# Fewer word halves decoded in attention's tail, an earlier maximum and a separate strip buffer in a fused attention, expert and channel-mix kernel

## The chip, the cores and the metric

The kernel runs on one core of a Trainium2 chip. The time is the device time of one execution in microseconds (us). TensorE is PE, VectorE is DVE, ScalarE is ACT, GpSimd is POOL, SyncE is SP; a q behind a name (SPq, POOLq) is the engine as one that issues DMAs. A product is one PE instruction of a stationary 128 x 128 tile with up to 512 moving columns.

## What is computed

Three layers follow each other on 2 x 768 tokens of width 512. The attention is local (96 tokens back) with 8 global keys; the second layer sends each token to one of eight experts (a route by argmax, held over where a local gate is at least 0.5); the third is a channel mix. Cut from the reference:

```python
a = softmax(mask(scale * q @ k.T + bias))          # 2 x 8 heads x 768 x 64
x = (a @ v)                                        # 2 x 768 x 512
# experts: e chosen token by token
h = np.maximum(x[b, s] @ w1[e], 0.0)               # 512 x 1024
out[b, s] = p[e] * (h @ w2[e])                     # 1024 x 512
# channel mix
xk = mu_k * x + (1.0 - mu_k) * x_prev              # x_prev: token before
xr = mu_r * x + (1.0 - mu_r) * x_prev
k = np.maximum(xk @ w_k, 0.0)                      # 512 x 1024
v = k * k @ w_v                                    # 1024 x 512
r = 1.0 / (1.0 + np.exp(-(xr @ w_r)))              # 512 x 512
return r * v
```

The weights of the third layer, w_k, w_v and w_r, come as float64.

## The kernel before

**Products in three parts.** Every float32 operand of a product is split into a rounded part and a remainder (names that end in h or hi, and l or lo), and a product is made of three: hi x hi (L637), lo x hi (L638) and hi x lo (L639), by `mm3`. The rounded part is made by ACT, the remainder by DVE, which needs ACT's result. Weights: whi by ACT (L616), wlo by DVE (L622, L630). Activations that were turned on PE (L643): L645 on ACT and L646 on DVE. A wait of PE at L639 for a DVE split is thus a wait for the remainder.

**Words.** The float64 weights are read as pairs of 32-bit words. There are 20 pieces (`PIECES`), each half of one 128 x 1024 tile and 512 KB of words. `dec_load` (L741) asks POOL's DMA queue for a piece; `decode_fast` makes float32 of it in three DVE steps (L485, L487, L489). Pieces 0 and 1 are decoded early in attention. Pieces 2 to `TAILED` - 1 are decoded one step a call by `D_` while attention runs out, with three buffers in turn (dwa, qz, vp); when a piece is decoded, its buffer takes the next request. The other pieces are decoded by `B_` during the expert tiles, with two buffers of the tag dw (dwt in the rows). The results lie in z0, in the four slots of a large tile, zbig, and in four z tiles. The program's order on each engine is the order in which these calls are written; DVE and POOL take their instructions strictly in that order.

**Fill.** Attention's routing must be complete before any expert but those rows that are known already. So two tiles of the first expert are computed inside attention's tail by a generator `fl`, which `F_(m)` advances by m steps; `D_` calls stand between them. etb is the activation that turns up there between the expert's two products. At the end the third tile of the first expert is fetched as x0 by SP (L1221), turned and split into x0s.

**Expert tiles.** After attention come the first expert's third tile, experts 1 to 7 and, in the last of them, the preparation of block 0 of the channel mix. `W_` splits weights ahead, `B_` decodes words, and tables of numbers (`W0`, `B0`, `BL`, `WS`, `W7`) say how many steps stand behind each group of products.

**Channel mix.** `stage3` runs six blocks of 256 tokens. Per block: eight `k_step` (12 products of 256 columns into a bank S, squared by ACT and DVE: sq, kh, kl), two `r_unit` (products into PT, a sigmoid) and two `v_unit` (products into O, the output o). Before it, a block's gathered rows yg are scaled (L1332), turned by PE into a strip (one column of the token before, then 256 tokens) and mixed with the column before: `mix_a` on POOL, `mix_b` on DVE (L1366), then split into xrh and xrl, xkh and xkl (L1372 on ACT, L1376 on DVE). `early(u)` does this for block 0, at the steps u that `EARLY_AT` lists in the order scale, turn, scale, ra, rb, hi, lo, turn, ra, rb, hi, lo, ka, kb, khi, klo, khi, klo. The strips of even and odd blocks lie in slots 0 and 1 of zbig, where slot 0 also holds the word tile c = 0: its strip can be written only when that tile's remainder (wlo_0) has been taken.

**Check of the words.** In blocks 1 to 3 `find_small` reads all pieces once more and writes a minimum per piece into `n.low`. In block 4 at k_step 6 `small_w3` takes the maximum over the pieces on DVE (w3top, L495), turns it on PE (L497) and compares it (L499, L500) for the flag that chooses the general path.

Of the kernel before, what the change touches and what calls it, by code (L numbers as in the profile page):

```python
# [37 lines left out]
SHORT = (3, 5)  # L38
TAILED = 10
CAPS = [384, 256, 256 + LAST] + [256] * 5  # L40
# [9 lines left out]
WNEXT = (0, 0, 0, 1, 2, 1, 1, 2, 1, 1, 1, 1, 1, 0, 0, 0)  # L50
EARLY_AT = (7, 9, 11, 12, 12, 12, 14, 11, 13, 13, 13, 14, 13, 14, 16, 18, 16, 19)


class Net:
# [426 lines left out]
    def decode_fast(self, dst, src):  # L481
# [8 lines left out]
        yield  # L490

    def small_w3(self, pool):
        nc = self.nc
        top = pool.tile([P, 1], F32, name="w3top")
        nc.vector.tensor_reduce(top, self.low, axis=AX.X, op=ALU.max)  # L495
        tp = self.bank("R", 1)
        nc.tensor.transpose(tp[0:1, 0:P], top, self.ident)  # L497
        one = pool.tile([1, 1], F32, name="w3one")
        nc.vector.tensor_reduce(one, tp[0:1, 0:P], axis=AX.X, op=ALU.max)  # L499
        nc.vector.tensor_scalar(one, one, -F64_MIN ** 2, None, op0=ALU.is_gt)  # L500
        self.badi = pool.tile([1, 1], I32, name="badi")
        nc.vector.tensor_tensor(self.badi, self.bad, one, op=ALU.max)
# [63 lines left out]
def build(ctx, tc, ins, out):  # L566
# [163 lines left out]
    w3 = {nm: ins[nm].bitcast(U32) for nm in ("w_k", "w_v", "w_r")}  # L730
    ZS = KD * TB + 8
    zbig = zp0.tile([P, PAIRS, ZS], F32, name="zbig")
    strip = zbig[:, :, 0:S]
    WORD = (8, 9, 0, 1, 2, 3, 4, 5, 6, 7)
# [20 lines left out]
    ndw = [0]  # L755
    zs = [zbig[:, j, :] for j in range(4)]

    def zslot(k_, m):
        return zs[k_][:, 0:m]
# [222 lines left out]
    with tc.manual_schedule():  # L982
# [4 lines left out]
        n.setup()  # L987
        peb = [ap.tile([P, 2 * P], F32, name=f"peb{i}") if i % 2 else zbig[:, i // 2, S:S + 2 * P] for i in range(8)]
        qzz = ap.tile([P, 2 * PAIRS * P], F32, name="qz")
# [197 lines left out]
        n.route_ri(g[1], stat[g[1]][1])  # L1187
        F_(2)
        emit_pv(NI - 1, 0)
        emit_pv(NI - 1, 1)  # L1190
# [30 lines left out]
        nc.sync.dma_start(out=x0[0], in_=n.xs[bass.ds(row, P), :])  # L1221
        for _ in fl:
            D_(2)
        for _ in dgen:
# [8 lines left out]

    zs += [zp.tile([P, ZS], F32, name=f"z{j}") for j in range(4)]

# [95 lines left out]
    def scale(t):  # L1331
        nc.vector.tensor_scalar(yg[t], yg[t], n.PE[:, t:t + 1], 1.0, op0=ALU.mult, op1=ALU.mult)  # L1332

    def strip(b):
        if b not in strips:
            strips[b] = zslot(b % 2, KD * (TB + 1)).rearrange("p (a c) -> p a c", a=KD)
        return strips[b]
# [150 lines left out]
    def stage3():  # L1488
        small = small_words()
        for b in range(NB):  # L1490
            a, l = prep(b + 1) if b + 1 < NB else ([], [])
            if b == 0:
                gather(2)
                gather(3)
                for f in (KF + KF, KF + KF + 1):
                    early(f)
                for i in range(2):
                    r_unit(b, i)
                    early(KF + KF + 2 + i)
                    W_(4)  # L1500
            for f in range(KF):
# [7 lines left out]
                if b == 0:  # L1509
                    W_(2)  # L1510
                elif b < 4:
                    next(small, None)
                elif b == 4 and f == 6:
                    n.small_w3(rp)
# [15 lines left out]
    WS = (2, 1, 2, 1, 2, 1, 2, 1) + (2, 2, 2, 2, 1, 1, 1, 1)  # L1530
    BL = {1: ((0,) * 8, 9), 2: ((1, 1, 1, 0, 1, 1, 1, 0), 4), 6: ((1, 1, 1, 0, 1, 1, 1, 0), 2)}
    LATE = 4
    W0 = (0,) * 8 + (2, 2, 2, 2, 1, 1, 1, 1)
    B0 = (0, 0, 0, 0, 0, 0, 1, 0, 1, 0, 1, 1, 0, 1, 0, 1)
    W7 = ((1, 0, 0, 0, 2, 1, 2, 0, 1, 2, 2, 1, 1, 0, 0, 0), (0, 0, 0, 0, 0, 2, 2, 4, 0, 0, 0, 2, 2, 0, 2, 2))

# [337 lines left out]
```

## Time and profile before

| | |
|---|---|
| median of 3 runs | 521.3 us (520.7 to 522.87) |
| the profiled execution's own time | 519.15 us |
| its span | 517.2 us |
| PE busy | 487.6 us, 94% |
| weight loads of PE, beside it | 412.4 us, 80% |
| DVE busy | 347.1 us, 67% |
| ACT busy | 260.3 us, 50% |
| POOL busy | 130.6 us, 25% |
| read from and written to memory | 73.75 MB and 12.98 MB |

The profiled execution is one of its own, with a time of its own, some 2 us longer than the span of its instructions. The places of the kernel in that span: attention to about 140 us, its tail and the fill to 158, the expert tiles to about 326, then the channel mix. Times in the rows are from the start of the span. Matmuls overlap, so that busy times of neighbours run into each other; how close they follow is read from their starts.

### The profile page before, as it was taken

What the parts mean: (1) busy time and instruction counts of PE and PEld (TensorE: products, weight loads), DVE (VectorE), ACT (ScalarE), POOL (GpSimd) and SP (SyncE); (2) the same over time, 40 slices, a digit from 0 to 9 for tenths busy, and PEclk for the clock granted to TensorE, in tenths of its full rate; (3) what the DMA queues carried; (4) which work ended last, traced back from release to release, by engine and by line L of the source; (5) the groups of instructions that cost most, each with busy time, mean ns of one, the idle gap of its engine ahead of it and who ended that gap; (6) DMA issues with size and microseconds to landing.
All of it is one profiled execution on the core that took longest, in us unless ns stands there. A gap on an engine that the chain in (4) does not pass through costs nothing. (4 is left out here: it accounts for less than half of the span.)

```text
span 517.2 us, 9297 instructions
## 1 busy us (share of the span) xinstructions
PE 487.6 (94%) x3231; PEld 412.4 (80%) x3231; DVE 347.1 (67%) x885; ACT 260.3 (50%) x627; POOL 130.6 (25%) x225
## 2 busy tenths in 40 slices
PE   7999999989868999999999999789999999979995
PEld 4788888867647989867978988588989899878985
DVE  6768697977865775847887954887766768353301
ACT  4876867846314654647667655663433414133220
POOL 4101211561210000000000001724562918161220
PEclk8999999999989999999999999999999999989998
DMA  8987687666386966599689722101736441200101
GB/s 162 257 216 162 150 158 233 198 216 228 113 280 216 323 206 240 189 347 302 209 306 298 293 100 62 41 23 61 286 111 217 160 171 55 82 0 1 41 4 46
DMA packets 77128, 87.43 MB, mean 169 GB/s; under 512 B 50960, under 2 KB 51216, under 8 KB 77072
## 3 DMA queue, kind: packets, MB, share of 16 engines
q1 hardware_dynamic: 68304, 63.28, 40.0%
q0 software_dynamic: 4800, 16.78, 9.9%
q10 hardware_dynamic: 3968, 6.69, 3.5%
q8 instruction: 28, 0.46, 0.4%
q14 instruction: 28, 0.23, 0.1%
HBM read 73.75 MB, written 12.98 MB: 168 GB/s over the span
## 5 line engine op out<-in xcount | busy, mean ns | idle before, releaser
L616 ACT ACTIVATE whi<-wraw 128x512 fp32r<-128x512 f32 x124 | 70.1, 623 | 8.2 <-ACTq L699 2.6
L630 DVE TENSOR_TENSOR wlo<-wraw,whi 128x1024 fp32r<-128x1024 f32 x55 | 65.8, 1216 | 12.2 <-ACT whi L616 12.2
L1398 ACT ACTIVATE sq<-S 128x256 f32<-128x256 f32 x48 | 18.5, 385 | 83.8 <-PE S L639 81.3
L638 PE MATMUL S<-xkl,whi 128*128 128x256 f32 x192 | 54.7, 285 | 1.4 <-DVE xkl L1376 1.4
L637 PE MATMUL S<-xkh,whi 128*128 128x256 f32 x192 | 55.7, 290 | 0.0
L639 PE MATMUL S<-xkh,wlo 128*128 128x256 f32 x192 | 54.7, 285 | 0.0
L1408 POOL TENSOR_TENSOR kl<-sq,kh 128x256 fp32r<-128x256 f32 x40 | 34.9, 881 | 78.0 <-ACT kh L1407 78.0
L1438 DVE TENSOR_TENSOR o<-O,sig 128x512 f32<-128x512 f32 (+1 forms) x13 | 8.5, 650 | 55.7 <-PE O L639 34.1
L639 PE MATMUL O<-whi,kl 128*128 128x512 f32 (+1 forms) x104 | 39.4, 379 | 0.2 <-DVE kl L1408 0.2
L638 PE MATMUL O<-wlo,kh 128*128 128x512 f32 (+1 forms) x104 | 39.3, 377 | 0.0
L637 PE MATMUL O<-whi,kh 128*128 128x512 f32 (+1 forms) x104 | 39.2, 377 | 0.0
L638 PEld LDWEIGHTS S<-xkl,whi 128*128 128x128 f32 x192 | 36.8, 192 | 1.9 <-DVE xkl L1376 1.6
L637 PEld LDWEIGHTS S<-xkh,whi 128*128 128x128 f32 x192 | 36.7, 191 | 0.3
L639 PEld LDWEIGHTS S<-xkh,wlo 128*128 128x128 f32 x192 | 36.7, 191 | 0.0
L1399 DVE SCALAR_TENSOR_TENSOR sq<-S,sq 128x256 f32<-128x256 f32 x48 | 20.1, 421 | 18.7 <-ACT sq L1398 18.0
L741 POOL DMA_DIRECT2D dwt<-in_moe_w_v_dram x8 | 4.2, 530 | 92.0 <-DVE z L489 68.6
L883 ACT ACTIVATE pt<-PT 128x512 f32<-128x512 f32 (+1 forms) x24 | 13.4, 557 | 25.7 <-PE PT L876 23.6
L637 PE MATMUL O<-whi,hh 128*128 128x512 f32 x64 | 25.3, 396 | 0.0
L639 PE MATMUL O<-whi,hl 128*128 128x512 f32 x64 | 25.3, 395 | 0.0
L638 PE MATMUL O<-wlo,hh 128*128 128x512 f32 x64 | 25.2, 394 | 0.0
L1407 ACT ACTIVATE kh<-sq 128x256 fp32r<-128x256 f32 x48 | 19.7, 412 | 10.3 <-DVE sq L1399 10.3
L867 ACT ACTIVATE zbig<-zbig,nm 128x232 f32<-128x232 f32 (+1 forms) x48 | 22.4, 467 | 2.3 <-DVE nm L855 1.7
(435 smaller groups left out, 1453.4 us busy)
## 6 DMA issues: line engine op xcount, KB each, us to landing
wraw<-in_moe_w_dram SPq DMA_DIRECT2D x64, 512.0 KB, 6.0
dwt<-in_moe_w_v_dram POOLq DMA_DIRECT2D x8, 512.0 KB, 6.5
z<-in_moe_w_k_dram SPq DMA_DIRECT2D x8, 512.0 KB, 5.7
z<-in_moe_w_v_dram SPq DMA_DIRECT2D x8, 512.0 KB, 4.1
ys<-yo ACTq DMA_DIRECT2D x15, 256.0 KB, 5.1
xn<-xs SPq DMA_DIRECT2D x14, 256.0 KB, 4.2
vn<-in_v_dram SPq DMA_DIRECT2D x12, 256.0 KB, 5.7
kn<-in_k_dram SPq DMA_DIRECT2D x11, 256.0 KB, 5.3
```

Of the source, the lines that this page charges most:

```text
L616: nc.scalar.activation(out=whl[r, c][0][:, sl], in_=raws[r, c][:, sl], func=ACTF.Copy)
L630: nc.vector.tensor_tensor(lo, raws.pop((r, c)), hi.bitcast(F32), op=ALU.subtract)
L637: nc.tensor.matmul(out_, lhsT=ah, rhs=bh, start=first, stop=False)
L638: nc.tensor.matmul(out_, lhsT=ah, rhs=bl, start=False, stop=False)
L639: nc.tensor.matmul(out_, lhsT=al, rhs=bh, start=False, stop=last)
L867: nc.scalar.activation(out=pe, in_=pe, func=ACTF.Exp, scale=-1.0, bias=nm[:, h:h + 1], accum_out=sm[:, h:h + 1])
L883: nc.scalar.activation(out=d[:, 0:ps.shape[1]], in_=ps, func=ACTF.Copy)
L1398: nc.scalar.activation(out=sq_, in_=ps[:, 0:TB], func=ACTF.Relu)
L1399: nc.vector.scalar_tensor_tensor(sq_, ps[:, 0:TB], 0.0, sq_, op0=ALU.max, op1=ALU.mult)
L1407: nc.scalar.activation(out=hh, in_=sq_, func=ACTF.Copy)
L1408: (nc.gpsimd if b else nc.vector).tensor_tensor(hl, sq_, hh.bitcast(F32), op=ALU.subtract)
L1438: nc.vector.tensor_tensor(o[:, a:z], ps[:, 0:z - a], sig[b, i][:, a:z], op=ALU.mult)
```

## The change

Four things are changed together. `TAILED` goes from 10 to 7: pieces 7, 8 and 9 are no longer decoded in the tail, but by `B_` in the expert tiles, and the tables `B0`, `BL` and `W7` give those steps places; the calls of `D_` in the tail stand elsewhere (one `D_(2)` more near its start, then 0, 0, 1, 1 in turn at its end instead of 2 every time). The maximum of the word check becomes a function of its own, `small_top`, and is called in block 4 at k_step 1; the transposition stays at k_step 6. The strip of block 0 gets a buffer of the tag dw, strips of later blocks stay in zbig, which is now laid out with rows of 258 (257 columns are used), and `EARLY_AT` has new steps. In `stage3` two weight steps stand ahead of the r units of block 0, and five instead of four behind each.

```diff
-TAILED = 10
+TAILED = 7
-EARLY_AT = (7, 9, 11, 12, 12, 12, 14, 11, 13, 13, 13, 14, 13, 14, 16, 18, 16, 19)
+EARLY_AT = (7, 9, 8, 11, 12, 12, 12, 11, 12, 13, 13, 13, 13, 14, 16, 18, 16, 18)
...
+    def small_top(self, pool):
+        self.top = pool.tile([P, 1], F32, name="w3top")
+        self.nc.vector.tensor_reduce(self.top, self.low, axis=AX.X, op=ALU.max)
...
-        top = pool.tile([P, 1], F32, name="w3top")
-        nc.vector.tensor_reduce(top, self.low, axis=AX.X, op=ALU.max)
+        top = self.top
...
-    ZS = KD * TB + 8
-    zbig = zp0.tile([P, PAIRS, ZS], F32, name="zbig")
+    ZW = TB + 2
+    zbig = zp0.tile([P, PAIRS, KD, ZW], F32, name="zbig")
...
         F_(2)
+        D_(2)
         emit_pv(NI - 1, 0)
...
-        for _ in fl:
-            D_(2)
+        for j, _ in enumerate(fl):
+            D_((0, 0, 1, 1)[j % 4])
...
+    def strip_tile(b):
+        if b:
+            return zbig[:, b % 2, :, 0:TB + 1]
+        return mp.tile([P, KD, TB + 1], F32, tag="dw", bufs=2, name="strip0")
...
+                W_(2)
                 for i in range(2):
                     r_unit(b, i)
                     early(KF + KF + 2 + i)
-                    W_(4)
+                    W_(5)
...
+                elif b == 4 and f == 1:
+                    n.small_top(rp)
                 elif b == 4 and f == 6:
                     n.small_w3(rp)
...
-    BL = {1: ((0,) * 8, 9), 2: ((1, 1, 1, 0, 1, 1, 1, 0), 4), 6: ((1, 1, 1, 0, 1, 1, 1, 0), 2)}
+    BL = {1: ((0, 0, 0, 0, 1, 0, 1, 0), 4), 2: ((1, 1, 1, 0, 1, 1, 1, 0), 3), 6: ((1, 1, 1, 0, 1, 1, 1, 0), 2)}
...
-    B0 = (0, 0, 0, 0, 0, 0, 1, 0, 1, 0, 1, 1, 0, 1, 0, 1)
+    B0 = (0, 0, 0, 0, 0, 0, 0, 1, 1, 0, 0, 1, 1, 1, 1, 0)
```

**The end of the fill.** On DVE, before, from the remainder of the fill's last weight on (wlo_0; the zbig rows are word steps, and the word after the arrow is the buffer they read):

```order
L622 TENSOR_TENSOR wlo_0_2110<-wraw_0_1938,whi_0_2109 128x512
L485 TENSOR_SCALAR zbig<-vp 128x512
L487 SCALAR_TENSOR_TENSOR zbig<-vp,zbig 128x512
L489 SCALAR_TENSOR_TENSOR zbig<-vp,zbig 128x512
L485 TENSOR_SCALAR zbig<-dwa 128x512
L646 TENSOR_TENSOR etb_2104<-PT_2189,etb_2103 128x512
L487 SCALAR_TENSOR_TENSOR zbig<-dwa,zbig 128x512
L489 SCALAR_TENSOR_TENSOR zbig<-dwa,zbig 128x512
```

and further on, to the split of x0:

```order
L646 TENSOR_TENSOR etb_2104<-PT_2220,etb_2103 128x512
L485 TENSOR_SCALAR zbig<-dwa 128x512
L487 SCALAR_TENSOR_TENSOR zbig<-dwa,zbig 128x512
L489 SCALAR_TENSOR_TENSOR zbig<-dwa,zbig 128x512
L485 TENSOR_SCALAR zbig<-qz 128x512
L487 SCALAR_TENSOR_TENSOR zbig<-qz,zbig 128x512
L489 SCALAR_TENSOR_TENSOR zbig<-qz,zbig 128x512
L646 TENSOR_TENSOR x0s<-T_2246,x0s 128x512
```

After, on DVE, the same place in one piece:

```order
L625 TENSOR_TENSOR wlo_0_2113<-wraw_0_1938,whi_0_2112 128x512
L649 TENSOR_TENSOR etb_2107<-PT_2186,etb_2106 128x512
L489 SCALAR_TENSOR_TENSOR zbig<-vp,zbig 128x512
L485 TENSOR_SCALAR zbig<-dwa 128x512
L649 TENSOR_TENSOR etb_2107<-PT_2209,etb_2106 128x512
L487 SCALAR_TENSOR_TENSOR zbig<-dwa,zbig 128x512
L489 SCALAR_TENSOR_TENSOR zbig<-dwa,zbig 128x512
L649 TENSOR_TENSOR x0s<-T_2231,x0s 128x512
L485 TENSOR_SCALAR zbig<-qz 128x512
```

Both splits of etb now stand ahead of the steps that they followed, and the split of x0 ahead of the qz word instead of behind the words of vp, dwa and qz; line numbers are larger by three. On POOL, the requests for words (L741, then L745) among the scatters of rows (L277), before:

```order
L277 DMA xs<-X_1537,posi 12288x512
L277 DMA xs<-X_1710,posi 12288x512
L741 DMA vp<-in_moe_w_k_dram 128x1024
L277 DMA xs<-X_1852,posi 12288x512
L277 DMA xs<-X_2031,posi 12288x512
L741 DMA dwa<-in_moe_w_k_dram 128x1024
L741 DMA qz<-in_moe_w_k_dram 128x1024
L741 DMA vp<-in_moe_w_k_dram 128x1024
L741 DMA dwa<-in_moe_w_k_dram 128x1024
L741 DMA qz<-in_moe_w_k_dram 128x1024
```

and after:

```order
L277 DMA xs<-X_1537,posi 12288x512
L277 DMA xs<-X_1710,posi 12288x512
L745 DMA vp<-in_moe_w_k_dram 128x1024
L745 DMA dwa<-in_moe_w_k_dram 128x1024
L277 DMA xs<-X_1852,posi 12288x512
L277 DMA xs<-X_2034,posi 12288x512
L745 DMA qz<-in_moe_w_k_dram 128x1024
L745 DMA dwt_2266<-in_moe_w_k_dram 128x1024
```

The second request into dwa has moved ahead of the last two scatters; the last requests into vp, dwa and qz are gone, and requests into dwt follow instead.

**The start of block 0.** On DVE, before, from the last expert's weight w_9 on (xmr, xmk: mixing; xrl, xkl: remainders; wlo_0 to wlo_3: splits of word tiles; yg: scaling):

```order
L622 TENSOR_TENSOR wlo_9_4390<-w_9_1969,whi_9_4389 128x512 x2
L1332 TENSOR_SCALAR yg_4354<-yg_4354,PEX 128x512
L622 TENSOR_TENSOR wlo_0_4404<-zbig,whi_0_4403 128x512 x2
L646 TENSOR_TENSOR ehl_4360<-PT_4416,ehh_4359 128x512
L1332 TENSOR_SCALAR yg_4356<-yg_4356,PEX 128x512
L1366 SCALAR_TENSOR_TENSOR xmr_4450<-zbig,mur,xmr_4450 128x128 x4
L622 TENSOR_TENSOR wlo_1_4444<-zbig,whi_1_4443 128x512 x2
L1366 SCALAR_TENSOR_TENSOR xmr_4450<-zbig,mur,xmr_4450 128x128 x4
L1376 TENSOR_TENSOR xrl_4460<-xmr_4450,xrh_4459 128x4x128 x2
L1366 SCALAR_TENSOR_TENSOR xmk_4476<-zbig,muk,xmk_4476 128x256 x4
L622 TENSOR_TENSOR wlo_2_4491<-zbig,whi_2_4490 128x512 x2
L1376 TENSOR_TENSOR xkl_4507<-xmk_4476,xkh_4506 128x512
```

and after:

```order
L625 TENSOR_TENSOR wlo_9_4393<-w_9_1940,whi_9_4392 128x512 x2
L1337 TENSOR_SCALAR yg_4357<-yg_4357,PEX 128x512
L1337 TENSOR_SCALAR yg_4359<-yg_4359,PEX 128x512
L625 TENSOR_TENSOR wlo_0_4407<-zbig,whi_0_4406 128x512 x2
L649 TENSOR_TENSOR ehl_4363<-PT_4420,ehh_4362 128x512
L1376 SCALAR_TENSOR_TENSOR xmr_4445<-strip_4427,mur,xmr_4445 128x128 x4
L1386 TENSOR_TENSOR xrl_4464<-xmr_4445,xrh_4463 128x4x128
L1376 SCALAR_TENSOR_TENSOR xmr_4445<-strip_4427,mur,xmr_4445 128x128 x4
L1386 TENSOR_TENSOR xrl_4464<-xmr_4445,xrh_4463 128x4x128
L1376 SCALAR_TENSOR_TENSOR xmk_4480<-strip_4427,muk,xmk_4480 128x256 x4
L625 TENSOR_TENSOR wlo_1_4439<-zbig,whi_1_4438 128x512 x2
L1386 TENSOR_TENSOR xkl_4505<-xmk_4480,xkh_4504 128x512 x2
```

The split wlo_1 has moved from between the two groups of mixing for r to behind the mixing for k, each xrl follows its own mixing, and the second yg stands ahead of wlo_0.

**Block 4.** On DVE, before, from the sq of k_step 3 on:

```order
L1399 SCALAR_TENSOR_TENSOR sq_3_5774<-S_5761,sq_3_5774 128x256
L1399 SCALAR_TENSOR_TENSOR sq_4_5800<-S_5787,sq_4_5800 128x256
L1399 SCALAR_TENSOR_TENSOR sq_5_5822<-S_5809,sq_5_5822 128x256
L1366 SCALAR_TENSOR_TENSOR zbig<-zbig,muk 128x256 x4
L1399 SCALAR_TENSOR_TENSOR sq_6_5846<-S_5833,sq_6_5846 128x256
L495 TENSOR_REDUCE w3top<-w3low 128x1
```

and after, from the sq of k_step 0 on:

```order
L1409 SCALAR_TENSOR_TENSOR sq_0_5711<-S_5698,sq_0_5711 128x256
L1337 TENSOR_SCALAR yg_5714<-yg_5714,PEX 128x512
L1409 SCALAR_TENSOR_TENSOR sq_1_5733<-S_5720,sq_1_5733 128x256
L494 TENSOR_REDUCE w3top<-w3low 128x1
L1337 TENSOR_SCALAR yg_5716<-yg_5716,PEX 128x512
L1409 SCALAR_TENSOR_TENSOR sq_2_5756<-S_5743,sq_2_5756 128x256
```

The reduction to w3top stood behind the four mixing operations and the sq of k_step 6; now it stands behind the sq of k_step 1. The order of PE and of SP's requests is the same in both kernels.

## Rows read from the trace of the kernel before

**Rows 1.** Page, 40 slices of the span: clock and DVE in tenths, memory rate

```profile
PEclk8999999999989999999999999999999999989998
DVE  6768697977865775847887954887766768353301
GB/s 162 257 216 162 150 158 233 198 216 228 113 280 216 323 206 240 189 347 302 209 306 298 293 100 62 41 23 61 286 111 217 160 171 55 82 0 1 41 4 46
```

**Rows 2.** Waits of PE: total us, times, longest

```profile
PE O L639 <- DVE etb L646: 3.8, 2, 3.3
PE S L639 <- DVE x0s L646: 3.1, 1, 3.1
PE R L497 <- DVE w3top L495: 2.6, 1, 2.6
```

**Rows 3.** Timeline of PE, 138 to 158: start, us, instruction, [idle before]

```profile
141.36 0.39 PE L638 MATMUL O<-wlo,etb 128*128 128x512 f32 x1
145.09 0.50 PE L639 MATMUL O<-whi,etb 128*128 128x512 f32 x1 [3.33 <-DVE etb L646]
...
151.63 0.60 PE L643 MATMUL T<-ident,x 128*128 128x128 f32 x4
...
153.00 0.39 PE L638 MATMUL O<-wlo,etb 128*128 128x512 f32 x1
153.23 0.39 PE L639 MATMUL O<-whi,etb 128*128 128x512 f32 x1
...
157.22 0.50 PE L639 MATMUL S<-whi,x0s 128*128 128x512 f32 x1 [3.13 <-DVE x0s L646]
```

**Rows 4.** Timeline of DVE, 138 to 158

```profile
144.01 0.43 DVE L485 TENSOR_SCALAR zbig<-dwa 128x512 uint32<-128x512 uint32 x1 [2.40 <-DMA dwa<-in_moe_w_k_dram]
...
144.95 0.68 DVE L487 SCALAR_TENSOR_TENSOR zbig<-dwa,zbig 128x512 uint32<-128x512 uint32 x1
...
154.68 0.43 DVE L485 TENSOR_SCALAR zbig<-qz 128x512 uint32<-128x512 uint32 x1 [2.12 <-DMA qz<-in_moe_w_k_dram]
...
156.48 0.68 DVE L646 TENSOR_TENSOR x0s<-T,x0s 128x512 fp32r<-128x512 f32 x1
```

**Rows 5.** Timeline of ACT, POOL and SP's queue, 138 to 158

```profile
139.94 0.60 ACT L645 ACTIVATE etb<-PT 128x512 fp32r<-128x512 f32 x1 [1.22 <-PE PT L643]
138.62 0.58 POOL L741 DMA_DIRECT2D dwa<-in_moe_w_k_dram  x1
140.52 0.34 SPq L1221 DMA_DIRECT2D x<-xs  x1
```

**Rows 6.** DMA issues: count, KB each, median us to landing

```profile
wraw<-in_moe_w_dram SPq DMA_DIRECT2D x64, 512.0 KB, 6.0
dwt<-in_moe_w_v_dram POOLq DMA_DIRECT2D x8, 512.0 KB, 6.5
...
xn<-xs SPq DMA_DIRECT2D x14, 256.0 KB, 4.2
```

**Rows 7.** Timelines of PE, ACT and DVE at block 0

```profile
331.54 0.50 PE L639 MATMUL PT<-whi,xrl 128*128 128x512 f32 x1 [2.23 <-DVE xrl L1376]
339.17 0.38 PE L638 MATMUL S<-xkl,whi 128*128 128x256 f32 x1 [1.40 <-DVE xkl L1376]
334.77 1.28 ACT L1422 ACT_TABLE_LOAD   x1
340.57 0.42 DVE L1399 SCALAR_TENSOR_TENSOR sq<-S,sq 128x256 f32<-128x256 f32 x1
```

**Rows 8.** Timelines of DVE and PE at block 4

```profile
459.96 2.61 DVE L1366 SCALAR_TENSOR_TENSOR zbig<-zbig,muk 128x256 f32<-128x256 f32 x4
460.25 0.28 PE L639 MATMUL S<-xkh,wlo 128*128 128x256 f32 x1
...
466.76 0.39 PE L637 MATMUL PT<-whi,xrh 128*128 128x512 f32 x1
```

**Rows 9.** Waits of DVE in the expert tiles: total us, times, longest

```profile
DVE z L485 <- DMA dwt<-in_moe_w_v_dram: 1.8, 1, 1.8
```

More of the change, by code (lines that the diff above doesn't have):

```diff
@@ L730, in build @@
     w3 = {nm: ins[nm].bitcast(U32) for nm in ("w_k", "w_v", "w_r")}
-    ZS = KD * TB + 8
-    zbig = zp0.tile([P, PAIRS, ZS], F32, name="zbig")
-    strip = zbig[:, :, 0:S]
+    ZW = TB + 2
+    zbig = zp0.tile([P, PAIRS, KD, ZW], F32, name="zbig")
+    zflat = zbig.rearrange("p j a c -> p j (a c)")
+    strip = zflat[:, :, 0:S]
     WORD = (8, 9, 0, 1, 2, 3, 4, 5, 6, 7)
@@ L755, in build @@
     ndw = [0]
-    zs = [zbig[:, j, :] for j in range(4)]
+    zs = [zflat[:, j, :] for j in range(4)]
     def zslot(k_, m):
@@ L987, in build @@
         n.setup()
-        peb = [ap.tile([P, 2 * P], F32, name=f"peb{i}") if i % 2 else zbig[:, i // 2, S:S + 2 * P] for i in range(8)]
+        peb = [ap.tile([P, 2 * P], F32, name=f"peb{i}") if i % 2 else zflat[:, i // 2, S:S + 2 * P] for i in range(8)]
         qzz = ap.tile([P, 2 * PAIRS * P], F32, name="qz")
@@ L1232, in build @@
     TILES = [(2,), (0, 1), (0, 1, 2)] + [(0, 1)] * 5
-    zs += [zp.tile([P, ZS], F32, name=f"z{j}") for j in range(4)]
+    zs += [zp.tile([P, 1024], F32, name=f"z{j}") for j in range(4)]
     def xtile(shape, c, name):
@@ L1332, in scale @@
         nc.vector.tensor_scalar(yg[t], yg[t], n.PE[:, t:t + 1], 1.0, op0=ALU.mult, op1=ALU.mult)
+    def strip_tile(b):
+        if b:
+            return zbig[:, b % 2, :, 0:TB + 1]
+        return mp.tile([P, KD, TB + 1], F32, tag="dw", bufs=2, name="strip0")
     def strip(b):
         if b not in strips:
-            strips[b] = zslot(b % 2, KD * (TB + 1)).rearrange("p (a c) -> p a c", a=KD)
+            strips[b] = strip_tile(b)
         return strips[b]
@@ L1530, in build @@
     WS = (2, 1, 2, 1, 2, 1, 2, 1) + (2, 2, 2, 2, 1, 1, 1, 1)
-    BL = {1: ((0,) * 8, 9), 2: ((1, 1, 1, 0, 1, 1, 1, 0), 4), 6: ((1, 1, 1, 0, 1, 1, 1, 0), 2)}
+    BL = {1: ((0, 0, 0, 0, 1, 0, 1, 0), 4), 2: ((1, 1, 1, 0, 1, 1, 1, 0), 3), 6: ((1, 1, 1, 0, 1, 1, 1, 0), 2)}
     LATE = 4
     W0 = (0,) * 8 + (2, 2, 2, 2, 1, 1, 1, 1)
-    B0 = (0, 0, 0, 0, 0, 0, 1, 0, 1, 0, 1, 1, 0, 1, 0, 1)
-    W7 = ((1, 0, 0, 0, 2, 1, 2, 0, 1, 2, 2, 1, 1, 0, 0, 0), (0, 0, 0, 0, 0, 2, 2, 4, 0, 0, 0, 2, 2, 0, 2, 2))
+    B0 = (0, 0, 0, 0, 0, 0, 0, 1, 1, 0, 0, 1, 1, 1, 1, 0)
+    W7 = ((1, 0, 0, 0, 2, 1, 2, 0, 1, 2, 2, 1, 1, 0, 0, 0), (0, 0, 0, 0, 0, 2, 2, 2, 2, 0, 2, 0, 0, 0, 0, 2))
     with tc.manual_schedule():
```

## The prediction

> **What bounds the kernel now.** I read the page's slices first: TensorE (PE) is busy 94% of the span, so a microsecond is worth something only where PE waits. The clock row shows two levels, 9 (2.4 GHz) and 8 where a slice holds a stretch at the lower level (1.2 GHz); there are four: the first and the last of the span, the twelfth (142 to 155 us) and the thirty-sixth (453 to 465) [rows 1]. Next, the waits of PE, sorted by size: the three largest are a split of etb (3.8 us in two waits), a split of x0s (3.1) and w3top (2.6) [rows 2]. All three end on VectorE (DVE). Last, the timelines around these three places. They tell why DVE was late.
>
> In the tail of attention PE starts a product at 141.36 and the next at 145.09, and later stops again from 153.70 or so until 157.22 [rows 3]. DVE explains both stops. At 144.01 it starts the first step of a word half that it had waited 2.40 us for, and at 154.68 another that it had waited 2.12 us for; both waits end with a DMA [rows 4]. DVE works in order: behind the first stands the second half of the etb split, which takes its input from ScalarE (ACT), and ACT's half had started at 139.94 and takes 0.60 [rows 5], so it had been ready at 140.54, over 3 us before. The x0s split stands behind the second word at 156.48 [rows 4]. So PE waits for a transfer that it doesn't need for 100 us yet. The word for 144.01 was requested at 138.62 only [rows 5].
>
> In block 4 of the last stage PE starts a product at 460.25 and then the transposition of w3top, after 2.6 us of wait; the reduction that makes w3top stands on DVE behind four mixing operations that start at 459.96 and take 2.61 us together [rows 2, 8].
>
> **Part A, words moved out of the tail.** Removed from the tail: three of the eight word halves that are decoded there, that is nine DVE steps, each set 0.43 + 0.68 + 0.68 = 1.8 us (two fused steps, of which one stands here) [rows 4], 5.4 us in all, and three loads of 512 KB. More important is the order: etb's split now stands ahead of the word that DVE waited for, x0s' split ahead of the second such word, and the request for the first word stands two scatters earlier on the POOL queue.
>
> What PE needs there: from 141.36 to 157.22 it takes 15.86 us [rows 3]. In it are 25 products, the one at 141.36 counted and the one at 157.22 not, and two groups of four transpositions. At full clock products start 0.23 apart (153.00 and 153.23), and a group takes at most the 0.60 of its row [rows 3]. 25 x 0.23 + 2 x 0.60 = 6.95. So 15.86 - 6.95 = 8.9 us can go, and this holds the 3.3, 0.4 and 3.1 of waits and some 2 us that the products between 145.1 and 148.8 ran at the lower clock behind the first stop (the 8 in the twelfth slice).
>
> What is late next: x0 itself. Its load is issued at 140.52, in both orders at the same place [rows 5]. By the 4.2 us of loads of the same shape it lands at 144.7; by the 6.0 of the larger weights at 146.5 [rows 6]. PE transposes it in the group that now starts at 151.63 [rows 3]; between 141.36 and that group lie 17 products and the other group, without the stops 17 x 0.23 + 0.60 = 4.5 us, so PE is there at 145.9. x0 is in time by 1.2 or late by 0.6; I take it in time, since 4.2 is from the same shape and queue. Gain 8.9, between 7.5 (x0 late by 0.6 and as much again for a stretch at the lower clock behind that stop) and 9.4 (if a group takes 0.35).
>
> What the nine steps cost where they go: into the expert tiles, 155 to 297 us, where DVE's digits (slices 13 to 23) are 5 7 7 5 8 4 7 8 8 7 9, a mean of 0.68 [rows 1]. That leaves some 0.32 x 142 = 45 us of idle DVE for 5.4 us. I cost them at nothing. The cover is DVE's lead over PE: if a weight split is late by one step, PE stands 0.4 to 0.7 each time. Loads: 1.57 MB more in that stretch, at a mean 266 GB/s over these slices; single slices carry up to 347 [rows 1], so queues have room. Cost nothing, between 0 and the whole of it (rival 1).
>
> **Part B, the first strip in its own buffer.** Block 0 may be mixed before word tile c = 0 has been split, so the mixing of block 0 moves ahead of one split pair on DVE and of the second scaling. Two waits of PE are touched: xrl, 2.23 us at 331.54, and xkl, 1.40 us at 339.17 [rows 7]. The xrl split now comes directly behind its own mixing, so the first wait should shrink to nothing. But the gain is not kept: the third step of block 0 needs the bank that the first sq operation frees, at 340.57 [rows 7], and the work on DVE ahead of it is the same in kind and number in both orders (same splits, same mixing, same scalings, only permuted), with DVE at 8 tenths in slices 26 and 27, 323 to 349 us [rows 1]. PE arrives earlier and waits there. ACT adds the table load, 1.28 us at 334.77 [rows 7], which sits ahead of a sigmoid and two splits in both orders. I take 0.3 kept, between -1.0 (the load moves ahead of a split that PE waits for) and +2.2 (the whole xrl wait). Row stride 258 instead of 257 of the zbig tile changes no count: nothing.
>
> The table load is where the Trainium skill ("ScalarE: Activation LUTs", section "What ACT_TABLE_LOAD costs") says more than the row: 1.28 us of load plus 1.38 us of drain, 2.66 for a switch. The load's row agrees with the first figure; a drain has no row here. By the page's price the splits behind it would come 1.4 later and B would be about -0.2, an estimate that moves the sum by half a microsecond.
>
> **Part C, the maximum of the word check.** The reduction (0.16 us or so) goes from step 6 to step 1 of block 4, ahead of the second scaling; the transposition stays at step 6. Its input, the table of minima, is complete after block 3. From 460.25 to 466.76 PE takes 6.51 us [rows 8]. It holds 13 products of 256 columns, three of 512 and the transposition. At full clock: 13 x 0.12 + 3 x 0.23 + 0.2 = 2.45. Gain 4.06, of which 2.6 is the wait and the rest the products behind it at the lower clock. What is late next? The sq of step 6 stands behind the four mixing operations in both orders, but PE needs it only in the v units, with step 7 and the r units of the block before them. I take 4.1, between 3.5 and 4.2. Adding 0.16 us on DVE at step 1 costs nothing, since DVE idles between its operations there.
>
> **Sum.** -8.9 - 0.3 - 4.1 = -13.3 us on the profiled execution: 519.15 - 13.3 = 505.85. That execution lies 2.15 below the median of three (521.3); I keep the offset and predict 508.0.
>
> **The rivals.**
> 1. *The 1.57 MB in the expert tiles make weights late.* If queues there were already full, 1.57 MB at 266 GB/s adds 5.9 us where PE is bound: 508.0 + 5.9 = 513.9. For it: slices of 298 to 347 GB/s [rows 1], and weights of 512 KB that need 6.0 us to land [rows 6]. Against: the slices of 189 and 209 beside them. Chance 0.10.
> 2. *The strip's gain is kept.* B at 2.2 instead of 0.3: 506.1. For it: the wait of 2.23 is real. Against: DVE's full queue up to 340.57. Chance 0.08.
> 3. *C is not gained.* Another operation keeps PE at step 6, or the reduction at step 1 is itself late: 512.1. Chance 0.05.
> 4. *Slower: DVE stands at the words in the expert tiles as it stood in the tail.* By the tables the tiles of experts 0 to 2 now take 6 + 6 + 15 = 27 steps, nine words, where it was 6 + 2 + 12; each would wait like the two in the tail, 2.1 to 2.4 us [rows 4], in front of weight splits. 9 x 2.3 = 20.7 us: 508.0 + 20.7 = 528.7. With two buffers a word is requested when the one before the last is decoded, so it decides when a load takes longer than DVE needs for one word and the splits beside it, and by more than the split behind it is early. For it: loads of this kind need 6.5 us [rows 6], and one of the ten words of the expert tiles waited 1.8 us already [rows 9]. Against: only one did, and PE did not wait for it. Chance 0.05. The Trainium skill ("SBUF — State Buffer", section "Who interferes with whom") has a rule for it: DVE and POOL share a pair of ports as an exclusive lock, and transfers queued by POOL can be starved while DVE holds it. By that rule more DVE word steps beside POOL's word loads would lengthen the landing. The landing times of the rows, 6.5 us from POOL's queue and 6.0 from SP's for the same size [rows 6], show no such starvation, so the rule's case has no more than this chance.
> 5. *The gain of A comes back in the experts in another way*, so that the time stays within 0.5%: chance 0.02.
>
> **How the numbers follow.** Forecast 0.70. A from 7.5 to 9.4, B from -1.0 to 2.2, C from 3.5 to 4.2, and the median of three itself spreads 0.6 below and 1.6 above. All at their good ends at once is unlikely: 504.5 as the low end takes 3.5 from the forecast, rival 2 lies inside. The high end, 512.5, takes in rival 3 and B and A at their bad ends. Outside are rivals 1, 4, 5 and the tails of the forecast, together about 0.2. The bound of 0.5% (2.6 us) is about what a measurement of this kernel can tell from no change. Faster by over 0.5%: 0.93; within: 0.02; slower: 0.05.
>
> **What would show it.** In the trace after: (A) no wait of PE over 0.5 us at etb or x0s, the x0s products starting about 9 us earlier against 141.36's product, and a clock digit of 9 there; a wait of PE for the transposition of x by a DMA would show x0 late. (B) the wait for xrl gone, and in its place one for a bank freed by sq at an unchanged distance from the start of block 0; if the block's later products have also come nearer to its first one, rival 2. (C) no wait for w3top, and 13 small products 0.12 apart. Rival 1: PE waiting for wlo or whi in experts 1 to 4. Rival 4: DVE waits at L485 for words, several of 2 us. The forecast is wrong if the sum of PE's waits in the expert tiles grows by over 3 us.

## The result, and the profile after

| | before | after |
|---|---|---|
| median, this comparison | 521.69 us (520.7 to 522.87, 4 runs) | 501.62 us (499.54 to 504.26, 4 runs) |
| ratio, 95% interval | | 0.9617 [0.956, 0.9674] |
| profiled execution, its span | 519.15, 517.2 | 503.04, 501.0 |
| DVE busy | 347.1 (67%) | 345.6 (69%) |
| PE busy | 487.6 (94%) | 481.4 (96%) |

20.1 us were gained where 13.3 were forecast (508.0), and the median lies 2.9 below the low end of the range. Two later comparisons on other chips gave 0.9628 [0.9598, 0.9659] and 0.9638 [0.96, 0.9677]. So the direction was right and the size was not.

The three rows of the page that answer to [rows 1], from the profile of the changed kernel:

```profile
PEclk9999999999799999999999999989999999999999
DVE  6778788896766875967887964898675948364311
GB/s 159 273 199 189 126 185 175 258 225 132 228 188 227 346 218 319 190 334 315 212 339 308 284 148 45 61 22 63 222 157 154 246 87 166 64 21 1 42 3 47
```

The lower clock has moved: the digits below 9 stand now in the eleventh slice (125 to 138 us) and in the twenty-seventh (326 to 338); those at the etb split and at w3top are gone. The waits of PE from 310 us to 345 us are these (total, times, longest); none at etb, x0s or w3top is left in the whole list, and xrl has none:

```profile
PE S L640 <- ACT whi L619: 0.7, 1, 0.7
PE S L641 <- DVE xkl L1386: 0.7, 1, 0.7
PE O L642 <- DVE ehl L649: 0.3, 1, 0.3
PE S L642 <- DVE wlo L625: 0.2, 1, 0.2
```

**Tail of attention.** The timeline of PE, with the product that stood at 141.36 in [rows 3], the transposition of x, and the product that stood at 157.22:

```profile
143.45 0.39 PE L641 MATMUL O<-wlo,etb 128*128 128x512 f32 x1
...
147.81 0.60 PE L646 MATMUL T<-ident,x 128*128 128x128 f32 x4
...
150.11 0.40 PE L642 MATMUL S<-whi,x0s 128*128 128x512 f32 x1
```

The stretch of 15.86 us takes 6.66, no wait in it. DVE tells why (its timeline there):

```profile
142.66 0.69 DVE L649 TENSOR_TENSOR etb<-PT,etb 128x512 fp32r<-128x512 f32 x1 [0.94 <-ACT etb L648]
143.27 0.68 DVE L489 SCALAR_TENSOR_TENSOR zbig<-vp,zbig 128x512 uint32<-128x512 uint32 x1
143.87 0.42 DVE L485 TENSOR_SCALAR zbig<-dwa 128x512 uint32<-128x512 uint32 x1
145.87 0.69 DVE L649 TENSOR_TENSOR etb<-PT,etb 128x512 fp32r<-128x512 f32 x1 [1.58 <-ACT etb L648]
...
149.13 0.69 DVE L649 TENSOR_TENSOR x0s<-T,x0s 128x512 fp32r<-128x512 f32 x1 [1.25 <-ACT x0s L648]
149.74 0.42 DVE L485 TENSOR_SCALAR zbig<-qz 128x512 uint32<-128x512 uint32 x1
```

DVE now waits for ACT's half of each split instead of for words, the word out of dwa has landed by 143.87 without a wait, and x0s is split before the qz word.

**Block 4.** The last product ahead of the transposition of w3top (460.25 in [rows 8]), the transposition, and the product that stood at 466.76:

```profile
449.11 0.28 PE L642 MATMUL S<-xkh,wlo 128*128 128x256 f32 x1
449.22 0.27 PE L500 MATMUL R<-ident,w3top 128*1 128x128 f32 x1
...
451.45 0.40 PE L640 MATMUL PT<-whi,xrh 128*128 128x512 f32 x1
```

6.51 us have become 2.34.

**Where the rest is.** The order of PE is the same in both kernels, so the same products can be found in every trace, and the time between two of them be compared. The table gives six stretches: A is 141.36 to 157.22 in the trace of before, then to 328.57 (expert tiles), to 341.31 (start of block 0), to 460.25 (blocks 0 to 4), to 466.76 (C), to 508.95 (blocks 4 and 5). Kernels below the second line are the experiments.

| kernel | to 141.36 | A | experts | block 0 | blocks 0-4 | C | blocks 4-5 |
|---|---|---|---|---|---|---|---|
| before | 141.36 | 15.86 | 171.35 | 12.74 | 118.94 | 6.51 | 42.19 |
| after | 143.45 | 6.66 | 169.42 | 13.11 | 116.47 | 2.34 | 41.38 |
| top_only | 143.87 | 14.37 | 171.36 | 13.89 | 119.04 | 2.35 | 42.26 |
| tail_only | 143.34 | 7.29 | 170.89 | 12.71 | 119.08 | 6.60 | 42.18 |
| strip_only | 141.48 | 14.67 | 169.13 | 12.64 | 116.47 | 5.25 | 41.38 |
| pad64 | 144.74 | 15.51 | 169.35 | 12.72 | 116.78 | 6.67 | 41.78 |
| after_again | 144.82 | 6.66 | 168.83 | 12.63 | 116.41 | 2.34 | 41.38 |
| after_back | 141.12 | 6.66 | 170.68 | 12.60 | 119.04 | 2.35 | 42.25 |
| after_zbig | 141.02 | 7.36 | 169.10 | 12.07 | 116.45 | 2.34 | 41.39 |

Between before and after: A -9.2, C -4.2, block 0 +0.4, and three stretches in which the change was said to cost or gain nothing: experts -1.9, blocks 0 to 4 -2.5, blocks 4 and 5 -0.8, together -5.2 us. Ahead of all of it the after execution is 2.1 behind, by a stretch at the lower clock from 131 to 138 us (windows of PE in the trace of after: start and end, length, busy times, then the granted clock, DMA share and GB/s):

```profile
130.00:132.00 2.00, 1.84 (x12) 1.46 (x10) 1.44 (x4) 0.60 (x1) 0.00 (x0) 0.85 0.40 162
132.00:134.00 2.00, 2.00 (x11) 1.67 (x12) 1.70 (x10) 0.00 (x0) 0.47 (x1) 0.50 0.00 0
136.00:138.00 2.00, 2.00 (x7) 1.26 (x6) 1.20 (x5) 1.15 (x2) 1.46 (x2) 0.50 0.34 131
```

0.50 is the level of 1.2 GHz, 1.00 that of 2.4; ahead of it PE had waited 1.22 us for a step of the routing (er, at 129.30). The -5.2 come without any wait; they come a little at every product. A product's row names its moving operand first and its stationary one second: in the products of 256 columns the activations move and the weights stand, in those of 512 columns it is the other way round. In the two timelines below (before first, after second) stand the first of 48 products of 512 columns in block 3, the first of the 36 of 256 columns that follow them without a break, and the last of those:

```profile
438.30 0.39 PE L637 MATMUL O<-whi,kh 128*128 128x512 f32 x1
...
449.46 0.28 PE L637 MATMUL S<-xkh,whi 128*128 128x256 f32 x1
...
453.66 0.28 PE L639 MATMUL S<-xkh,wlo 128*128 128x256 f32 x1
```

```profile
427.77 0.39 PE L640 MATMUL O<-whi,kh 128*128 128x512 f32 x1
...
438.75 0.28 PE L640 MATMUL S<-xkh,whi 128*128 128x256 f32 x1
...
442.75 0.28 PE L642 MATMUL S<-xkh,wlo 128*128 128x256 f32 x1
```

Before: 11.16 us / 48 = 232.5 ns and 4.20 / 35 = 120 ns from start to start. After: 10.98 / 48 = 228.8 and 4.00 / 35 = 114. The clock is at its full level in both.

### The profile page after: what moved, and what is told of

Its sections match the earlier page's. It is cut to its first block, busy times and chain, and to the rows that moved or that the text cites. A ratio compares the mean times of both kernels' runs of the same rounds, so it can differ in the third digit from the quotient of the medians.

```text
span 501.0 us, 9283 instructions
## 1 busy us (share of the span) xinstructions
PE 481.4 (96%) x3231; PEld 408.6 (82%) x3231; DVE 345.6 (69%) x885; ACT 260.2 (52%) x627; POOL 131.2 (26%) x225
## 5 line engine op out<-in xcount | busy, mean ns | idle before, releaser
L1409 DVE SCALAR_TENSOR_TENSOR sq<-S,sq 128x256 f32<-128x256 f32 x48 | 20.1, 420 | 14.4 <-ACT sq L1408 14.1
L729 ACT ACTIVATE yo<-O 128x512 f32<-128x512 f32 (+1 forms) x16 | 9.5, 596 | 26.4 <-PE O L642 26.4
```

The lines of the kernel that those rows point to most:

```text
L1409: nc.vector.scalar_tensor_tensor(sq_, ps[:, 0:TB], 0.0, sq_, op0=ALU.max, op1=ALU.mult)
```

## The experiments

No kernel leaves out or changes any part of the computation. "Spacing" is the one of the two timelines above, in the same place of block 3 and 4.

### The parts alone, and the tiles moved

**top_only**: before, with part C.

```diff
+                elif b == 4 and f == 1:
+                    n.small_top(rp)
                 elif b == 4 and f == 6:
```

> The kernel before with part C alone (the maximum at k_step 1). Theory: the wait for w3top and the lower clock behind it go, 4.1 us less (ratio 0.990 to 0.994), and the pace of the products elsewhere stays that of before. Rival (PE is kept there by something else): 0 to 1.5 us less.

Measured: 516.65 us against 520.35, ratio 0.9936 [0.9906, 0.9966]. Stretch C 6.51 to 2.35, spacing 120 and 232 as before. The theory of part C holds: 3.7 us in the median, 4.2 in the stretch.

**tail_only**: before, with part A.

```diff
-TAILED = 10
+TAILED = 7
...
-        for _ in fl:
-            D_(2)
+        for j, _ in enumerate(fl):
+            D_((0, 0, 1, 1)[j % 4])
```

> The kernel before with part A alone (seven pieces in the tail, calls and tables as in the change), tiles in the places of before. Theory: 8.9 us less (7.5 to 9.4, ratio 0.982 to 0.986), all of it between 141 and 158 us, nothing given back in the expert tiles, pace of the products as before (119 ns for 256 columns). Rival (the products in the last stage are faster because words were moved): the changed pace, 113 to 114 ns, appears here, and the time falls by 13 to 14 us.

Measured: 512.06 against 520.35, 0.9836 [0.9791, 0.988], so -8.3. Stretch A 15.86 to 7.29; the expert tiles gave nothing back (171.35 to 170.89); spacing as before. The faster products are not an effect of the moved words.

**pad64**: before, with nothing but a wider slot for two buffers that the products never read.

```diff
-        return mp.tile([P, 1024], F32, tag="dw", bufs=2, name=f"dwt{ndw[0]}")
+        return mp.tile([P, 1028], F32, tag="dw", bufs=2, name=f"dwt{ndw[0]}")[:, 0:1024]
```

> The kernel before, and only the two dw buffers of the expert pool are declared 1028 instead of 1024 columns wide, of which 1024 are used: every tile that is placed behind them in that pool (xh, xl, hh, hl, xkh, xkl, xrh, xrl, kh, kl, the moving operands of the products) lies 64 bytes higher, as in the changed kernel. No instruction is moved. Theory (place of the tiles sets the pace of the products): products of 256 columns start 113 to 114 ns apart instead of 119, those of 512 columns 229 instead of 232, and the time falls by 4 to 6 us (ratio 0.988 to 0.992). Rival (the pace differs from run to run or chip to chip, or came with the strips or the words): spacing stays at 119, time within 1 us of before (ratio 0.998 to 1.002).

Measured: 514.63 against 520.35, 0.9903 [0.987, 0.9936], -5.7 us, with no instruction moved. Its timeline in the place shown above:

```profile
437.76 0.39 PE L637 MATMUL O<-whi,kh 128*128 128x512 f32 x1
...
448.74 0.28 PE L637 MATMUL S<-xkh,whi 128*128 128x256 f32 x1
...
452.74 0.28 PE L639 MATMUL S<-xkh,wlo 128*128 128x256 f32 x1
```

10.98 / 48 = 228.8 and 4.00 / 35 = 114 ns: the spacing of the changed kernel. Experts, blocks 0 to 4 and the end lose 2.0, 2.2 and 0.4 us. The buffer strip0 of 4112 bytes a row makes the two slots of the tag dw larger than the 4096 bytes of the words (the built program sets them 4128 apart), and all tiles placed behind them in the pool slide by 64 bytes; that is the missing term. The expectation calls xh to kl the moving operands; they are the activations of the products, moving with 256 columns and stationary with 512. Tiles that only other engines use slide with them (xn, yg and others), and no run separates whether the pace comes from PE's own reads or from what the other engines read and write beside them.

**strip_only**: before, with part B (buffer, rows of 258, early steps, weight steps).

```diff
+        return mp.tile([P, KD, TB + 1], F32, tag="dw", bufs=2, name="strip0")
```

> The kernel before with part B alone (own buffer for strip 0, rows of 258, early steps, weight steps of block 0 and the last expert as in the change). The buffer is 4112 bytes a row, so it moves the tiles by the same 64 bytes. Theory: it gains what the shift of the tiles gains, 4 to 6 us, and its own part is 0.3 us (-1 to 1): equal to the kernel with the shifted tiles alone. Rival (strip's gain kept): 2.2 us below the kernel with the shifted tiles alone. Rival (pace not by the place of tiles, but by the strip's rows of 258): gains 4 to 6 us where the shifted tiles alone gain nothing.

Measured: 511.62 against 520.35, 0.9864 [0.982, 0.9907]; 2.0 us below pad64 by the ratios (3.0 by the medians), but in the table the two differ by 0.1 in block 0. Most of what else they differ by lies ahead of A and in A and C, which neither touches, and where the executions differ in their stretches at the lower clock; strip_only has none behind its wait for w3top, pad64 has one. So the medians were no proof of a gain of the strip; this was tried again (after_zbig, zbig_mix).

### How the place of the tiles acts

Four kernels put a gap of so many bytes ahead of the expert pool of the kernel before, with one run each (the kernel before ran once beside them, at 519.67 us). With 128 bytes:

```diff
+    mp.tile([P, 32], F32, tag="gap", bufs=1, name="gap")
```

> The same with 32 bytes: operands at 32 modulo 64. If the place modulo 128 or 64 sets the pace: 119 ns or more, and the expert tiles' spacing for 512 columns at 232 or more.

> The kernel before with a gap of 128 bytes ahead of the expert pool, no instruction moved. Moving operands of the products then begin at 64 modulo 128, as in the kernel before (192 bytes past a multiple of 256 there, 64 past here). If the place modulo 128 sets the pace: 119 ns between products of 256 columns, as before. If any other place than that of before is fast: 113 to 114.

> The same with 192 bytes: operands at 0 modulo 128, but 128 modulo 256. If a multiple of 128 is enough: 113 to 114 ns. If a multiple of 256 or more is wanted: 119.

> The same with 320 bytes: operands at 0 modulo 256, but 256 modulo 1024. If a multiple of 128 or 256 is enough: 113 to 114 ns. If only 1024 (the bytes that one product of 256 columns reads in a partition) will do: 119.

Then, in the changed kernel, a gap of 192 bytes that takes the activations back to the residue of before, that is to the same place modulo 256 (**after_back**), and a gap ahead of the weights that moves these by 192 bytes, with one of 64 that brings the activations back to a multiple of 256 (**after_wgap**):

```diff
+    wp.tile([P, 48], F32, tag="gapw", bufs=1, name="gapw")
...
+    mp.tile([P, 16], F32, tag="gap", bufs=1, name="gap")
```

> The changed kernel with a gap of 192 bytes ahead of the expert pool, so that the operands of the products begin again 192 bytes past a multiple of 256, as in the kernel before; no instruction is moved. Theory (their place sets the pace): 119 and 232 ns again, and 4 to 6 us longer than the changed kernel. Rival (the pace came with the changed order): 113 to 114 ns, same time within 1.5 us.

> The changed kernel with the weight tiles (whi, wlo, wraw) moved up by 192 bytes, from 64 past a multiple of 256 to a multiple of 256, the moving operands staying at multiples of 256. If only the place of the moving operands counts: 113 to 114 and 229 ns, same time within 1.5 us. If the distance between weights and moving operands counts (then equal, as with the gap of 128): 120 ns for 256 columns and 227 for 512, some 2 us longer. If weights at a multiple of 256 are better by themselves: below 113 or 227 ns, 2 to 4 us shorter.

What these texts call moving operands are the activations, in either role. In the table the distance is where activations begin, less where weights begin, modulo 256, as the built programs place them (weights begin 64 past a multiple of 256, in after_wgap at one). Counted as the moving operand's place less the stationary one's, it is this distance with 256 columns and minus this distance with 512.

| kernel | distance | 512 columns, ns | 256 columns, ns | time |
|---|---|---|---|---|
| before, after_back | 128 | 232.5 | 120 | after_back 505.06 us, 0.9721 [0.9675, 0.9767] |
| shift32 | 160 | 233.3 | 117 | 522.25 us, one run |
| after, pad64, shift320 | 192 | 228.8 | 114 | shift320 516.10 us, one run |
| shift128, after_wgap | 0 | 226.7 | 120 | shift128 516.74 us, one run; after_wgap 503.15 us, 0.9675 [0.9635, 0.9716] |
| shift192 | 64 | 233.3 | 118 | 521.71 us, one run |

after_back's timeline, in the same place, shows the spacing of before in the changed order:

```profile
428.15 0.39 PE L640 MATMUL O<-whi,kh 128*128 128x512 f32 x1
...
439.31 0.28 PE L640 MATMUL S<-xkh,whi 128*128 128x256 f32 x1
...
443.51 0.28 PE L642 MATMUL S<-xkh,wlo 128*128 128x256 f32 x1
```

and after_wgap's that the weights' place counts too:

```profile
426.87 0.39 PE L641 MATMUL O<-whi,kh 128*128 128x512 f32 x1
...
437.75 0.28 PE L641 MATMUL S<-xkh,whi 128*128 128x256 f32 x1
...
441.94 0.28 PE L643 MATMUL S<-xkh,wlo 128*128 128x256 f32 x1
```

The simple expectation of shift192 (a multiple of 128 will do) falls, and so does the one that only the activations' own residue counts: the activations of after and after_wgap both begin at multiples of 256, and 256 columns take 114 in one and 120 in the other. In this place kernels with the same distance agree in both columns; as a rule that rests on one pair, shift128 and after_wgap, since in the other rows of several kernels activations and weights each lie at the same places modulo 256. after_back stands 0.0093 of the kernel before above the changed kernel's 0.9628 on the same chip, 4.8 us (3.2 between the medians of six runs each); its stretches in the table say 5.4 (1.9 + 2.6 + 0.9).

**after_mix**: the changed kernel with kh, kl, hh, hl (512 columns) at distance 0 and the other operands at 192, to have the better of both rows.

```diff
+        mp.tile([P, 16], F32, tag="gapa", bufs=1, name="gapa")
         hn = [mp.tile([P, D], F32, tag="h" + c, bufs=5, name=f"hn0{c}") for c in "hl"]
+        mp.tile([P, 48], F32, tag="gapb", bufs=1, name="gapb")
```

> The changed kernel with two gaps in the expert pool: hh, hl, kh, kl (operands of 512 columns of the second products) lie 64 bytes past a multiple of 256, as the weights do, and xh, xl, xkh, xkl, xrh, xrl stay at multiples of 256. Theory (distance from the weights modulo 256: 192 is best for 256 columns, 0 for 512): 113 to 114 ns for 256 columns as in the changed kernel, 227 instead of 227 to 232 for O products by hh, hl, kh, kl; some 454 products by 2.5 ns, 1.1 us shorter. Rival (one pool's place governs all): 120 ns for 256 columns, 2 us longer.

> The changed kernel unaltered, beside the two above on their chip: 0.960 to 0.966 of the kernel before.

Measured: 502.22 us, 0.9654 [0.9627, 0.9682], beside 501.15, 0.9638 [0.96, 0.9677] for the changed kernel (after_third). The products by kh and kl took 227 ns as expected, but those of 256 columns 118 in the place of the timelines (means of 115 to 118 from block to block), with their distance modulo 256 unchanged. No gain.

So the distance is not the whole of it, and two other kernels of this record show more. In pad64 and after_zbig (described below) every operand of every product of the channel mix lies at the same address. In the place of the timelines their spacing is the same, 228.8 and 114 ns. Further on, in blocks 4 and 5, it is not: here are the first of 48 products of 512 columns, and the first and the last of 96 of 256 columns that follow them without a break, pad64 first and after_zbig second.

```profile
470.72 0.39 PE L637 MATMUL O<-whi,kh 128*128 128x512 f32 x1
...
481.70 0.28 PE L637 MATMUL S<-xkh,whi 128*128 128x256 f32 x1
...
492.89 0.28 PE L639 MATMUL S<-xkh,wlo 128*128 128x256 f32 x1
```

```profile
453.24 0.40 PE L640 MATMUL O<-whi,kh 128*128 128x512 f32 x1
...
464.44 0.28 PE L640 MATMUL S<-xkh,whi 128*128 128x256 f32 x1
...
475.23 0.28 PE L642 MATMUL S<-xkh,wlo 128*128 128x256 f32 x1
```

pad64: 10.98 / 48 = 228.8 and 11.19 / 95 = 117.8 ns. after_zbig: 11.20 / 48 = 233.3 and 10.79 / 95 = 113.6. The granted clock is 1.00 in both. Among the kernels with all activations at distance 192, those with a stretch at the lower clock shortly before, in block 4 (in pad64 the granted clock is 0.89 from 455 to 470 us, in after_zbig 1.00 from 440 to 455), take 229 and 118 ns here (pad64, shift320), and those without take 233 and 114 (strip_only, after, after_zbig): what PE did before seems to count, which is read from these traces and not tried. So the place of the tiles sets the pace only in part, for both sizes; what else counts stays open.

### Whether the strip's buffer gains

**after_again** is the changed kernel unaltered, for comparison; **after_zbig** is the changed kernel with strip 0 in zbig again, early and weight steps as before, and the slots of dw kept wide, so that the tiles stay where they are; **zbig_mix** is that with the gaps of after_mix.

```diff
     def strip_tile(b):
-        if b:
-            return zbig[:, b % 2, :, 0:TB + 1]
-        return mp.tile([P, KD, TB + 1], F32, tag="dw", bufs=2, name="strip0")
+        return zbig[:, b % 2, :, 0:TB + 1]
```

> The changed kernel unaltered, on the chip and beside the kernels it is compared with here. Expected: 0.960 to 0.967 of the kernel before; the sum of the parts measured alone (words -8.3, maximum -3.7, strip with its shift of the tiles -8.7 us) is -20.7, so 499.5 to 503. If the parts overlapped, less: 503 to 507.

> The changed kernel without part B alone: strip 0 in zbig again, early steps and weight steps of block 0 and of the last expert as before; the tiles stay where the changed kernel has them. If the strip's own part is worth what was predicted (0.3 us, -1 to 1): within 1.3 us of the changed kernel. If its gain is kept (xrl wait of 2.2 us, and the stretch at the lower clock behind it of 1.7 us in some executions): 2 to 4 us longer.

> The same gaps in the changed kernel without part B (strip 0 in zbig). Theory: 1 to 2 us shorter than the changed kernel, for the places 1.1 and for the strip left out 0 to 1. Rival (strip's own part gains): longer than the kernel with the gaps and the strip by 1 to 3 us.

Measured: after_again 501.91, 0.9628 [0.9598, 0.9659], as the parts add up (0.0164 + 0.0064 + 0.0136 less than 1 is 0.9636). after_zbig 500.63, 0.9611 [0.9574, 0.9647]; zbig_mix 499.62, 0.9629 [0.959, 0.9669], against after_mix 0.9654. Both times the kernel without part B is 0.2% lower, inside the intervals; in the table its block 0 takes 12.07 against 12.63 us. The strip's buffer has no gain of its own. The two kernels without it are as fast as the changed one; none is shown to beat it.

## Why the prediction was right or wrong

**Part A, right.** Forecast 8.9, measured 9.2 in the stretch, inside 7.5 to 9.4, and 8.3 alone. x0 came in time: no wait ahead of the transposition at 147.81. The nine steps cost nothing in the expert tiles: PE waits there for no split. One word wait is longer than in [rows 9] (waits of DVE, 150 to 316 us, after):

```profile
DVE z L485 <- DMA dwt<-in_moe_w_v_dram: 4.6, 1, 4.6
```

so rival 4 has its mechanism, once, at a place where DVE had the time. The rule of the Trainium skill ("SBUF — State Buffer", section "Who interferes with whom"), by which transfers that POOL queues can be starved, does not show here: words from POOL's queue landed in 5.4 us (w_v) and 6.9 (w_k), weights from SP's in 5.8.

**Part B, right in kind, and in size by luck.** Forecast -0.3; measured +0.4 in the first profile, which has a stretch at the lower clock there (0.67 from 328 to 332 us), and -0.1 in after_again, which has none. The wait for xrl is gone and the one that was named, for the bank that the first sq frees, stands in its place, beside the halved one for xkl (1.40 in [rows 7]) and one for whi that was not named, in the waits of PE of after_again from 310 to 345 us:

```profile
PE S L640 <- ACT whi L619: 0.7, 1, 0.7
PE S L641 <- DVE xkl L1386: 0.7, 1, 0.7
PE S L640 <- DVE sq L1409: 0.7, 1, 0.7
```

That sq starts 12.2 us after the product that begins the stretch, where it was 12.0 before (340.57 in [rows 7], less 328.57). But after_zbig, without part B, has the wait for xrl, and yet takes 12.07 us instead of 12.63:

```profile
PE PT L642 <- DVE xrl L1384: 1.8, 1, 1.8
```

There that sq starts after 11.4 us. So the strip's buffer with its order cost 0.6, and something else, which the prediction put at nothing, gave about as much (below); the -0.1 is what was left of the two.

As for the drain that the Trainium skill ("ScalarE: Activation LUTs", section "What ACT_TABLE_LOAD costs") adds to the table load: after loads from 326.51 to 327.79, and the sigmoid starts at 327.80. The load's 1.28 us agree, no drain shows in the timeline of ACT here:

```profile
326.51 1.28 ACT L1432 ACT_TABLE_LOAD   x1
327.80 0.60 ACT L1432 ACTIVATE sig<-PT 128x512 f32<-128x512 f32 x1
```

**The step that failed: part B was priced by the order of its instructions alone.** The new buffer got no price for its size, and the layout of zbig got "Row stride 258 instead of 257 of the zbig tile changes no count: nothing." I looked at the instructions that a buffer's size changes and not at what is placed behind it. The new 4112-byte strip in a slot of 4096 moves the activations of nearly all products of the expert tiles and the channel mix by 64 bytes, while the weights stay where they were, worth 5.2 us in the trace and 5.7 alone. (zbig itself kept its size, 4 x 258 = 4 x 256 + 8, and moved nothing.) No term of the sum and no bound held it; a price for "all tiles behind it move" would have had to be there, as an unknown of either sign (shift32 and shift192, at 522.25 and 521.71 beside 519.67, were not faster than before, by one run each).

The other half of that step is smaller: with zbig declared in four dimensions, POOL's mixing of the first half of block 0 no longer stops behind its first operation for the second transposed half, which it doesn't read. tail_only's POOL first (flat rows), after_zbig's second (rows of 258):

```profile
317.59 0.38 POOL L1362 TENSOR_SCALAR xmr<-zbig,mur 128x128 f32<-128x128 f32 x1 [0.73 <-ACT zbig L1347]
319.18 3.53 POOL L1362 TENSOR_SCALAR xmr<-zbig,mur 128x128 f32<-128x128 f32 x7 [1.21 <-ACT zbig L1347]
```

```profile
313.97 4.13 POOL L1369 TENSOR_SCALAR xmr<-zbig,mur 128x128 f32<-128x128 f32 x8 [0.63 <-ACT zbig L1354]
```

From the start of the stretch, POOL is done with these eight operations after 1.2 us in tail_only and after 0.6 in after_zbig, about what block 0 gained. That the 12.07 us of after_zbig come from it is argued from these rows, and from pad64 and tail_only, whose block 0 gains nothing (12.72 and 12.71); it was not tried alone.

**Part C, right.** Forecast 4.1, measured 4.2 in the stretch, 3.7 alone.

**The offset, mis-sized.** I kept the 2.15 us between the profiled execution and the median. The one of after lies 1.4 above its median, that of before 2.5 below the later median of 521.69: 4.0 us between them. Stretches at the lower clock can account for that: they come behind a stop of PE, and not in every execution behind the same (in the table, top_only has one in block 0 and takes 13.89 us there, tail_only has none and takes 12.71). In the comparison with after_again the mean granted clock was 0.9805 over 11 runs of before and 0.9947 over 6 of the changed kernel, (0.0195 x 519) - (0.0053 x 501) = 7.5 us of clock loss less, if PE had work all that time; the sum held two stretches of it, some 3.4. That the stops which were removed had triggered more of it, on average, than the one profile of before showed, is argued: beside 0.9835 for the kernel before, the mean is 0.9888 with part A alone and 0.9856 with part C alone.

Together: 13.3 + 5.2 (tiles) + 4.0 (offset) - 2.1 (lower clock ahead of A in the profile of after) - 0.7 (block 0) + 0.4 (A and C) = 20.1. Either of the two misses alone, the 5.2 or the 4.0, would have left the time inside the range, whose low end lies 2.9 above it; it took both.

**Rivals.** Rival 1 (weights late) did not come: no wait for whi or wlo in experts 1 to 4. Rival 2 (strip kept) is refuted by block 0, though the total fell on its side. Rivals 3, 4, 5 did not come.

## What to carry to other kernels

When a change alters the size of any buffer, list which tiles of the same pool lie behind it and by how many bytes they move; the products may change pace without one instruction being moved, and only start-to-start distances show it, not the waits; read them in more than one block, since the places alone did not set them here. Compare stretches between the same instructions in two traces, not totals: here they separated effects that one median mixes. Behind a stop of PE count the lower clock as a chance taken over several executions, not as what one profile happens to show.

## What the runs showed of the hardware

In one place of the channel mix, products of float32 operands started 226.7 to 233.3 ns apart with 512 columns and 114 to 120 with 256, at one granted clock, with the distance between the addresses of the activations and of the weights modulo 256; the distance that is best for 512 columns (0) is among the worst for 256. With all addresses of the products the same, two traces still differed in blocks 4 and 5, by 228.8 against 233.3 and 117.8 against 113.6. Why, and why the 256-column products of after_mix did not keep their 114, stays open.
